# The first two blocks of rows handled in parts, and one transfer in place of two for the last weight rows

## The chip, the cores and the metric

The kernel runs on one NeuronCore of a Trainium2 chip. The metric is the device time of one execution in microseconds (us); lower is better. A NeuronCore has a matrix engine (PE, whose weight loads are shown apart as PEld), a vector engine (DVE), a scalar engine (ACT), GpSimd (POOL) and a sync engine (SP) that here only issues transfers. Each engine works through its own instruction list in order. DMA transfers are issued by SP, ACT and POOL, each on a queue of its own, and all queues are served by the same 16 DMA engines.

## The reference

```python
xn = layernorm(x)                                  # x = A_q, 2048 rows of 576
k_shift = sum_t k_pad[:, t:t+S] * shift_k[:, 3-t]  # causal convolution of 4 taps
kv = k_shift * v
y = irfft(rfft(kv, 2S) * rfft(ssm_k, 2S))[:S] + kv * ssm_D
out = x + xn * y + relu(xn @ w1) @ w2              # w1: 576 x 4608, w2: 4608 x 576
```

All data is float32. The feed-forward part (`relu(xn @ w1) @ w2`) is most of the work; the long convolution runs beside it.

## The kernel before, in words

The rows are taken in blocks of 512 (`BT` = 4 tiles of 128 rows). The first half of the rows is blocks 0 and 1, which are the tiles 0 to 3 and 4 to 7. The 4608 hidden columns are taken in 18 chunks of 256 (`FC`), each in two halves f = 0 and f = 1 of 128. Each chunk runs once for each half of the rows: 36 passes g.

To keep float32 precision every operand is split in a high part (cast to fp32r, named `hi`, `h` or index 0) and a low part (the difference, index 1). A product is then three matmuls: high by high, high by low, low by high. The 576 inputs are four pieces c = 0 to 3 of 128 and a rest of 64; for the rest the high and the low part of x lie one under the other in one operand of 128 partitions (`hl`), so the 64 rest rows of `w1` must stand twice over in `r1[:, 4, :]`.

The start (the first 33 us) is written out by hand:

- `load_acc` brings pairs of x tiles. The pair of tiles 0 and 1 and that of tiles 2 and 3 come first: each pair is two transfers of 64 partitions, one issued by SP and one by ACT. Then SP issues `load_w1(0)` (the weights of chunk 0, in four transfers), the pairs 4, 5 and 6, 7, and two `w2` tiles.
- `block_rows` centres the rows (`xn`), on DVE (statistics, then a subtraction: tiles 0, 2, and in block 1 tiles 4, 6, 7) or on ACT (tiles 1, 3 and 5).
- `block_xT` turns a block with PE transposes into PSUM tiles (`psx`: two tiles of two banks, and one `psf`), casts each piece on ACT to the high part (L304, rest L305) and subtracts it on DVE for the low part (L307, L308); then ACT copies the pieces out in float32 (`xf`) for later sums. `keep_warm` puts matmuls on nothing between the transposes.
- `split_w` casts weights to their high part on ACT (L529) and makes the low part on POOL (L530).
- `classical(g, b, f, ...)` writes the 14 matmuls of one half f of a chunk for block b: 12 on pieces, 2 on the rest. `hidden` makes the two parts of the relu on ACT (`hh`, L608) and DVE (`ll`, L613). For chunk 0, block 0 the order is `classical(0, 0, 0)`, then `classical(0, 0, 1)`, then the transposes of block 1 and the two halves of block 1; after them the first second-layer matmuls (`mm2`, tiles `pso`).

`tc.issue_after` fixes the order of two instructions on one engine without a wait. Passes 1 to 35 take their weights by `load_w1(g)` on POOL's queue, one pass ahead.

Of the kernel before, what the change touches and what calls it, by code (L numbers as in the profile page):

```python
# [12 lines left out]
AF = mybir.ActivationFunctionType  # L13
OP = mybir.AluOpType
# [3 lines left out]
P = 128  # L18
# [8 lines left out]
FT = 2  # L27
# [12 lines left out]
GR = P // (2 * A2)  # L40
NG = A1 // GR
N_WARM = 22
N_BETWEEN = 6
LATE = (0, 1, 5)


# [54 lines left out]
def h3_ffn_kernel(ctx: ExitStack, tc, x, k, v, shift_k, ssm_k, ssm_D, w1, w2, fwd, inv, mid, out):  # L101
# [41 lines left out]
    def fft_psum():  # L143
        return ps_f.tile([P, 512], F32, tag="f", name="psf")
# [17 lines left out]
    def halves(u):  # L162

        return slice(u * A1, (u + 1) * A1), slice((1 - u) * A1, (2 - u) * A1)
# [5 lines left out]
                with tc.issue_after(behind.ins):  # L170
                    behind = nc.sync.dma_start(kt_n[h, :, d:d + KD, :], src)

    def move(tile_, rows, t, store=False, queues=(nc.sync, nc.sync)):
        for u in range(U):
            a, b = tile_[halves(u)[0]], rows[u, :, t]
            last = queues[u].dma_start(*((b, a) if store else (a, b)))
        return last

# [95 lines left out]
    def block_rows(pool, b):  # L274

        xn = rows_tiles(pool, b)
        last = {t: done["low"] if b else None for t in (-2, -1)}
        for t in range(BT):
            last[t] = centre(xn[t], acc[b * BT + t], b * BT + t, CENTRED[b][t],
                             done["copied"] if b and t == 1 else last[t - 1 - (t < 3 or not b)])  # L280
        done["centred"] = last[BT - 1]
        return xn

    def block_xT(pool, b, names, tags, xn):

        wide = [ps_o.tile([P, 2, 512], F32, tag=f"o{k}", name=f"psx{b}{k}") for k in range(2)]
        ps = [wide[c // 2][:, c % 2, :] for c in range(4)] + [fft_psum()]
        if b == 0:
            transposed(ps, xn, [(c, t) for t in range(2) for c in range(5)])
            with tc.issue_after(done["pe"].ins):  # L290
                done["pe"] = keep_warm(N_BETWEEN)
            transposed(ps, xn, [(c, t) for c in range(5) for t in range(2, BT)])
        else:
            transposed(ps, xn, [(c, t) for c in range(5) for t in range(BT)])
        behind = done["centred"] if b == 0 else done["low"]
        for o, tag in zip(names, tags):
            operand(o, tag)
        rest_operand(b)
        with tc.issue_after(behind.ins):
            if b == 0:  # L300
                split_a(0)
            dst = [xo[names[c // 2]][:, :, c % 2, :] for c in range(4)]
            for c in range(4):
                nc.scalar.activation(dst[c][:, 0], ps[c], AF.Copy)  # L304
            high = nc.scalar.activation(hl[b][:64], ps[4][:64], AF.Copy)  # L305
            for c in range(4):
                nc.vector.tensor_tensor(dst[c][:, 1], ps[c], dst[c][:, 0], OP.subtract)  # L307
            done["low"] = nc.vector.tensor_tensor(hl[b][64:], ps[4][:64], hl[b][:64], OP.subtract)  # L308
        with tc.issue_after(high.ins):
            if b == 0:  # L310
                split_r(0)
                split_b(0)
                split_d(0)
            for o, src in zip(names, wide):
                xf[o] = pool.tile([P, 2, 512], F32, tag=f"xf{o}", name=f"xf{o}")
                nc.scalar.activation(xf[o], src, AF.Copy)  # L316
            xf[b] = pool.tile([64, 512], F32, tag=f"xfr{b}", name=f"xfr{b}")
            done["copied"] = nc.scalar.activation(xf[b], ps[4][:64], AF.Copy)
        if b:
            with tc.issue_after(done["low"].ins):  # L320
                for t in range(2 * BT):
                    if CENTRED[t // BT][t % BT] == "act":
                        stats(t, acc[t])
# [181 lines left out]
    def load_w1(g):  # L505
        queue = nc.gpsimd if g else nc.sync
        f = slice((g % NQ) * FC, (g % NQ + 1) * FC)
        r1 = wp.tile([P, 5, FC], F32, tag="r1", name=f"r1_{g}")
        for n in range(1 if g else 2):
            to = slice(0, FC) if g else slice(n * P, n * P + P)  # L510
            queue.dma_start(r1[:, :4, to], w1[:4 * P, f][:, to].rearrange("(c p) f -> p c f", p=P))
            if n == 0:
                for h in range(2):
                    queue.dma_start(r1[64 * h:64 * h + 64, 4, :], w1[4 * P:, f])
        raw1[g] = r1

    def load_w2(g, j):
# [7 lines left out]
    def split_w(g, kind, src, shape, bufs=1):  # L525
        w = wp.tile([P, 2, *shape], F32R, tag=kind, name=f"{kind}{g}", bufs=bufs)
        n = src.shape[1]
        with at_turn(g):
            nc.scalar.activation(w[:, 0, :n], src, AF.Copy)  # L529
        nc.gpsimd.tensor_tensor(w[:, 1, :n], src, w[:, 0, :n], OP.subtract)  # L530
        return w

# [86 lines left out]
    def classical(g, b, f, n_low, posted=0, upto=None):  # L619

        ps = bank(g, f, f"c{b}{f}")
        parts = ((wa[g], 0, wa[g], 2), (wb[g], 0, wd[g], 0))[f]
        names = (("00", "01"), ("10", "11"))[b]
        seq, late = [], []
        firsts, lasts = [], []
        for k in range(2):
            w, off = parts[2 * k:2 * k + 2]
            for c in range(2):
                h, l = w[:, 0, off + c, :], w[:, 1, off + c, :]
                hi, lo = xo[names[k]][:, 0, c, :], xo[names[k]][:, 1, c, :]  # L630
                seq += [(h, hi), (h, lo)]
                late.append((l, hi))
                if len(late) > LATE[n_low]:
                    seq.append(late.pop(0))
                if firsts:
                    firsts.insert(-1, (h, hi))
                    firsts.append((l, hi))
                else:
                    firsts = [(h, hi), (l, hi)]
                lasts.append((h, lo))  # L640
        if g == f == 0:
            seq, late = firsts + lasts, []
        seq.append((wr[g][:, 0, 0, f * P:(f + 1) * P], hl[b]))
        late.append((wr[g][:, 1, 0, f * P:(f + 1) * P], hl[b]))
        seq += late
        matmuls(ps, seq, True)
        tick(14 * W_MM)
        hidden(g, b, f, ps)
        post(posted, upto)

    def quad(g, units):

# [632 lines left out]

    warm = const.tile([P, 512], mybir.dt.bfloat16, name="warm")
    nc.vector.memset(warm, 0.0)
    for t in range(0, BT, 2):
        load_acc(t, queues=(nc.sync, nc.scalar))
    load_w1(0)  # L1290
    load_acc(BT)
    load_acc(BT + 2)
# [7 lines left out]
    def keep_warm(n):  # L1300
        for i in range(n):
            last = nc.tensor.matmul(idle[0], warm[:, :P], warm, start=True, stop=True)
        return last

    done["pe"] = keep_warm(N_WARM)
    with tc.tile_pool(name="fa", bufs=1) as fa:
        block_xT(fa, 0, ("00", "01"), (None, None), block_rows(fa, 0))
        xn = block_rows(fa, 1)
        classical(0, 0, 0, 1)
        classical(0, 0, 1, 2)  # L1310
        block_xT(fa, 1, ("10", "11"), ("s4", None), xn)
        load_w1(1)
        with tc.issue_after(done["low"].ins):
            inv_std(0, 2 * BT)
        with tc.issue_after(done["centred"].ins):
            for j in range(FT):
                split_w2(0, j)
                load_w2(1, j)
        classical(0, 1, 0, 0)
        split_a(1)  # L1320
        classical(0, 1, 1, 0)
        split_r(1)
        split_b(1)
        split_d(1)
        load_w1(2)
        spread_scales(fa)

        def unit(g, b, i, upto):
            mm2(g, b, i)
            post(1, upto)  # L1330

        for g in range(1, PLAIN):
            now = "00" if g < PLAIN - 1 else "10"
            for f in range(FT):
                for i in range(2):
                    unit(g - 1, 0, 2 * f + i, "00")
                if g == f == 1:
                    posts["at"] = second_half_of_start(fa)
                classical(g, 0, f, 0, 3, now if f else "00")
            for j in range(FT):  # L1340
                split_w2(g, j)
                load_w2(g + 1, j)
            for i in range(BT):
                unit(g - 1, 1, i, now)
            classical(g, 1, 0, 0, 3, now)
            split_a(g + 1)
            if g + 1 == PLAIN:
                sums(g + 1)
            split_r(g + 1)
            classical(g, 1, 1, 0, 3, None if g == PLAIN - 1 else now)  # L1350
            split_b(g + 1)
            split_d(g + 1)
            load_w1(g + 2)
        quad(PLAIN, [(PLAIN - 1, b, i) for b in range(2) for i in range(BT)])
        post(99)
# [38 lines left out]
```

## Time and profile before

| | |
|---|---|
| median of 3 runs | 1012.85 us (1012.47 to 1013.08) |
| the profiled execution, its own time | 1012.76 us |
| its span in the profile | 1011.0 us |
| PE busy | 1003.3 us (99%) |
| DVE, ACT, POOL busy | 685.9, 439.2, 442.5 us |
| POOL's rest-row transfers (L514) | 70, 36.7 us on POOL |

Between the span and the profiled execution's own time lie 1.8 us that the profile does not show. In the tables of stretches, each row gives for one stretch of the span the busy time and number of instructions of PE, PEld, DVE, ACT and POOL, the granted PE clock, the share of the 16 DMA engines, and GB/s. In timelines a row gives start, length, engine, line, operation, tiles, count, and in brackets the idle time before it with what ended it. In waits a row gives who waited for whom: total us, times, longest.

### The profile page before, as it was taken

Reading aid. Unit: us, or ns where it says so; the run is one execution under the profiler, and the core shown is the slowest. Engines: PE = TensorE matmul, PEld = TensorE weight load, DVE = VectorE, ACT = ScalarE, POOL = GpSimd, SP = SyncE. Lnnn points to the kernel's source line nnn. Section 1 sums busy time; section 2 is a strip of 40 time slices with the busy share of each in tenths; the row PEclk is TensorE's granted clock in tenths of the full one; section 3 lists DMA queues with packets and bytes.
Section 4 is the critical chain, followed back from the end, with each engine's and each line's share of the span. In section 5 each row is a group of like instructions: output and inputs, shape, how many; then the busy total and the mean of one; then the engine's idle time right before and its main releaser. Section 6 shows DMA issues by size and latency. Waiting matters only on the chain.

```text
span 1011.0 us, 17382 instructions
## 1 busy us (share of the span) xinstructions
PE 1003.3 (99%) x6502; PEld 844.4 (84%) x6502; DVE 685.9 (68%) x1057; ACT 439.2 (43%) x772; POOL 442.5 (44%) x500
## 2 busy tenths in 40 slices
PE   9999999999999999999999999999999999999998
PEld 5898999998878998898888888877777777787787
DVE  5787678875666676676767678556667666656774
ACT  7244444543554444444444444544454544432121
POOL 4335444554444744444444444334433244344450
PEclk9999999999999999999999999999999999999999
DMA  6654887771667534449863343478888987877954
GB/s 171 144 100 117 176 194 195 256 250 50 182 190 207 185 90 128 126 144 360 242 202 95 120 126 97 160 204 235 241 250 243 280 265 214 230 236 231 287 177 117
DMA packets 131032, 189.94 MB, mean 188 GB/s; under 512 B 69202, under 2 KB 83924, under 8 KB 130052
## 3 DMA queue, kind: packets, MB, share of 16 engines
q1 hardware_dynamic: 114564, 135.54, 47.0%
q0 software_dynamic: 15952, 52.40, 17.3%
q8 instruction: 51, 0.84, 0.3%
q10 hardware_dynamic: 432, 0.89, 0.3%
q14 instruction: 33, 0.27, 0.1%
HBM read 124.28 MB, written 50.34 MB: 173 GB/s over the span
## 4 chain that ended last, share of the span: by engine, by line
PE 97%; ACT 1%; DMA 1%; DVE 0%; issue 0%; ACTq 0%; DVEq 0%
PE pso L586 45%; PE psh L586 38%; PE psg L824 5%; PE psf L824 5%; PE psh_c L586 3%; DMA acc<-in_x 1%; ACT x L304 0%; DVE x L307 0%; PE psf L586 0%; ACT w L529 0%; ACT wb L529 0%; ACT xf L316 0%; ACT xs L224 0%; DVE bn L190 0%; ACT hh L608 0%
## 5 line engine op out<-in xcount | busy, mean ns | idle before, releaser
L586 PE MATMUL pso<-w,hh 128*128 128x288 f32 x2296 | 465.0, 296 | 0.0
L586 PEld LDWEIGHTS pso<-w,hh 128*128 128x128 f32 x2296 | 376.8, 188 | 30.8 <-ACT area L1134 6.5
L586 PE MATMUL pso<-w,ll 128*128 128x288 f32 x1148 | 338.4, 295 | 0.0
L811 DVE TENSOR_TENSOR acc<-pso,acc 128x576 f32<-128x576 f32 x237 | 178.7, 755 | 158.6 <-PE pso L586 158.2
L586 PEld LDWEIGHTS pso<-w,ll 128*128 128x128 f32 x1148 | 215.5, 188 | 0.0
L530 POOL TENSOR_TENSOR wb<-sums,wb 128x512 fp32r<-128x512 f32 x33 | 45.7, 1384 | 278.9 <-ACT wb L529 252.2
L530 POOL TENSOR_TENSOR w<-r,w 128x576 fp32r<-128x576 f32 x72 | 105.9, 1478 | 108.2 <-ACT w L529 107.9
L586 PE MATMUL psh<-xs,wb 128*128 128x512 f32 x396 | 102.4, 393 | 0.0
L586 PE MATMUL psh<-x,wa 128*128 128x512 f32 x396 | 102.2, 393 | 0.1
L613 DVE SCALAR_TENSOR_TENSOR ll<-psh,hh 128x512 fp32r<-128x512 f32 x66 | 45.5, 689 | 70.2 <-ACT hh L608 70.0
L586 PE MATMUL psh<-hl,wr 128*128 128x512 f32 x264 | 85.1, 403 | 0.0
L586 PEld LDWEIGHTS psh<-x,wa 128*128 128x128 f32 x396 | 72.4, 188 | 15.0 <-issue 0.4
L586 PEld LDWEIGHTS psh<-xs,wb 128*128 128x128 f32 x396 | 70.7, 188 | 12.1 <-issue 0.8
L711 ACT ACTIVATE psh<-psh 128x512 f32<-128x512 f32 x33 | 19.2, 582 | 137.7 <-DVE u L709 137.7
L530 POOL TENSOR_TENSOR wa<-r,wa 128x512 fp32r<-128x512 f32 x36 | 47.9, 1332 | 54.9 <-ACT wa L529 54.8
L824 PE MATMUL psg<-area 64*64 64x512 f32 (+10 forms) x632 | 64.1, 472 | 0.0
L586 PEld LDWEIGHTS psh<-hl,wr 128*128 128x128 f32 x264 | 46.0, 188 | 19.0 <-issue 10.4
L608 ACT ACTIVATE hh<-psh 128x512 fp32r<-128x512 f32 x66 | 39.2, 594 | 52.1 <-PE psh L586 51.8
L1114 DVE TENSOR_TENSOR area<-psf,area 128x512 f32<-128x512 f32 x72 | 44.7, 683 | 12.5 <-PE psf L824 8.1
L586 PE MATMUL psh<-x,wc 128*128 128x512 f32 x198 | 51.2, 394 | 0.0
L824 PE MATMUL psf<-area 64*64 64x512 f32 (+10 forms) x528 | 51.1, 451 | 0.0
L586 PE MATMUL psh<-xs,wc 128*128 128x512 f32 x198 | 51.0, 392 | 0.0
(144 smaller groups left out, 1436.2 us busy)
## 6 DMA issues: line engine op xcount, KB each, us to landing
r<-in_w POOLq DMA_DIRECT2D x70, 288.0 KB, 4.0
area<-area SPq DMA_DIRECT2D x144, 128.0 KB, 4.7
r<-in_w POOLq DMA_DIRECT2D x35, 512.0 KB, 4.9
zk<-area SPq DMA_DIRECT2D x64, 144.0 KB, 2.5
area<-zk SPq DMA_DIRECT2D x18, 512.0 KB, 4.6
area<-zx SPq DMA_DIRECT2D x18, 512.0 KB, 4.9
zy<-area SPq DMA_DIRECT2D x18, 512.0 KB, 2.9
area<-zy SPq DMA_DIRECT2D x32, 288.0 KB, 7.2
```

Source lines behind the costliest of these rows:

```text
L530: nc.gpsimd.tensor_tensor(w[:, 1, :n], src, w[:, 0, :n], OP.subtract)
L586: last = nc.tensor.matmul(ps, a, m, start=start and n == 0, stop=n == len(seq) - 1, skip_group_check=True)
L608: done["act"] = nc.scalar.activation(hh, ps, AF.Relu)
L613: done["ll"] = nc.vector.scalar_tensor_tensor(ll, ps, 0.0, hh, op0=OP.max, op1=OP.subtract)
L711: nc.scalar.activation(x, y, AF.Copy, scale=-1.0)
L811: done["acc"] = nc.vector.tensor_tensor(two(acc[t]), whole, two(acc[t]), OP.add)
L824: done["pe"] = nc.tensor.matmul(ps, a, m, start=start, stop=stop, skip_group_check=True)
L1114: nc.vector.tensor_tensor(filt[c][:, k, :], banks[k], filt[c][:, k, :], OP.mult)
```

## The change

What it does, part by part:

1. In `load_acc(2)` the second 64 partitions of the pair 2, 3 are loaded in two parts: 32 by ACT's queue, 32 by SP's.
2. `block_xT` gives each piece c = 0, 1, 2 a PSUM tile of its own (`psf`, half of a wide tile, `psf`); piece 3 and the rest share the second wide tile. The transposes of a block's first two tiles go first, for block 1 too; those of the last two go piece by piece, and the ACT cast and the DVE subtraction of a piece are written right behind its transposes. The `xf` copies are four of 512 columns, where there were two of 1024. `N_BETWEEN` goes from 6 to 3.
3. The high part of chunk 0's `wa` is made by DVE, where ACT made it.
4. The two halves of chunk 0 are written together (`first_chunk`), so that matmuls of the second half stand between those of the first. The casts of the first `w2` tiles on ACT move behind the casts of block 1.
5. In `load_w1` of every pass the 64 rest rows come by one transfer that reads them twice (its source has the dimensions 2, 64 and 256, the first with step 0), where two transfers of 64 rows came.

On PE, chunk 0 of block 0: `x_206` and `x_207` (after: `x_181`, `x_182`) are pieces 0, 1 and 2, 3 of block 0; `psh_c_260` is half f = 0, `psh_c_279` (after: `psh_c_261`) half f = 1; `hl` and `wr` are the rest. Before:

```order
L586 MATMUL psh_c_260<-x_206,wa_209 128x512 x2
L586 MATMUL psh_c_260<-x_207,wa_209 128x512 x2
L586 MATMUL psh_c_260<-hl_208,wr_222 128x512 x2
L586 MATMUL psh_c_279<-x_206,wb_225 128x512 x4
L586 MATMUL psh_c_279<-x_207,wd_228 128x512 x4
L586 MATMUL psh_c_279<-hl_208,wr_222 128x512
```

After:

```order
L599 MATMUL psh_c_260<-x_181,wa_197 128x512 x2
L599 MATMUL psh_c_260<-x_182,wa_197 128x512 x2
L599 MATMUL psh_c_261<-x_181,wb_223 128x512 x2
L599 MATMUL psh_c_261<-x_182,wd_226 128x512 x2
L599 MATMUL psh_c_260<-hl_183,wr_220 128x512 x2
L599 MATMUL psh_c_261<-x_181,wb_223 128x512 x2
```

Four matmuls of the second half now stand ahead of the two on the rest of the first half.

On ACT, between the relu parts of block 0 and the casts of block 1 (`w` is a `w2` tile, `x_321` or `x_302` is an operand of block 1). Before:

```order
L608 ACTIVATE hh_0_1_294<-psh_c_279 128x512
L529 ACTIVATE w_363<-r_0_0_123 128x576
L529 ACTIVATE w_368<-r_0_1_125 128x576
L304 ACTIVATE x_321<-psx_298 128x512 x2
L304 ACTIVATE x_322<-psx_299 128x512 x2
L305 ACTIVATE hl_323<-psf 64x512
```

After:

```order
L621 ACTIVATE hh_0_1_294<-psh_c_261 128x512
L307 ACTIVATE x_302<-psf 128x512
L307 ACTIVATE x_302<-psx_298 128x512
L307 ACTIVATE x_303<-psf 128x512
L307 ACTIVATE x_303<-psx_299 128x512
L307 ACTIVATE hl_304<-psx_299 64x512
L542 ACTIVATE w_335<-r_0_0_123 128x576
L542 ACTIVATE w_340<-r_0_1_125 128x576
```

The two `w2` casts moved behind the five casts of block 1.

On SP, the first transfers (`acc_109` is the pair 2, 3, `acc_117` the pair 4, 5, `r_0` chunk 0 of `w1`). Before:

```order
L176 DMA acc_109<-in_x 64x1152
L511 DMA r_0_112<-in_w 128x4x128
L514 DMA r_0_112<-in_w 64x256 x2
L511 DMA r_0_112<-in_w 128x4x128
L176 DMA acc_117<-in_x 64x1152 x2
```

After:

```order
L179 DMA acc_109<-in_x 64x1152
L177 DMA acc_109<-in_x 32x1152
L522 DMA r_0_113<-in_w 128x4x128
L524 DMA r_0_113<-in_w 128x1x256
L522 DMA r_0_113<-in_w 128x4x128
L179 DMA acc_117<-in_x 64x1152 x2
```

One x transfer is added ahead of the weights, and the rest rows are one row of the list.

```diff
-N_BETWEEN = 6
+N_BETWEEN = 3
...
-    def move(tile_, rows, t, store=False, queues=(nc.sync, nc.sync)):
+    def move(tile_, rows, t, store=False, queues=(nc.sync, nc.sync), part=A1):
         for u in range(U):
             a, b = tile_[halves(u)[0]], rows[u, :, t]
+            if u and part < A1:
+                queues[0].dma_start(a[part:], b[part:])
+                a, b = a[:part], b[:part]
             last = queues[u].dma_start(*((b, a) if store else (a, b)))
...
         wide = [ps_o.tile([P, 2, 512], F32, tag=f"o{k}", name=f"psx{b}{k}") for k in range(2)]
-        ps = [wide[c // 2][:, c % 2, :] for c in range(4)] + [fft_psum()]
-        if b == 0:
-            transposed(ps, xn, [(c, t) for t in range(2) for c in range(5)])
-            with tc.issue_after(done["pe"].ins):
-                done["pe"] = keep_warm(N_BETWEEN)
-            transposed(ps, xn, [(c, t) for c in range(5) for t in range(2, BT)])
-        else:
-            transposed(ps, xn, [(c, t) for c in range(5) for t in range(BT)])
+        ps = [fft_psum(), wide[0][:, 0, :], fft_psum(), wide[1][:, 0, :], wide[1][:, 1, :]]
...
+        transposed(ps, xn, [(c, t) for t in range(2) for c in range(5)])
+        if b == 0:
+            with tc.issue_after(done["pe"].ins):
+                done["pe"] = keep_warm(N_BETWEEN)
...
-            for c in range(4):
-                nc.scalar.activation(dst[c][:, 0], ps[c], AF.Copy)
-            high = nc.scalar.activation(hl[b][:64], ps[4][:64], AF.Copy)
-            for c in range(4):
-                nc.vector.tensor_tensor(dst[c][:, 1], ps[c], dst[c][:, 0], OP.subtract)
-            done["low"] = nc.vector.tensor_tensor(hl[b][64:], ps[4][:64], hl[b][:64], OP.subtract)
+        for cs in ((0,), (1,), (2,), (3, 4)):
+            transposed(ps, xn, [(c, t) for c in cs for t in range(2, BT)])
+            with tc.issue_after(behind.ins):
+                for c in cs:
+                    to = dst[c][:, 0] if c < 4 else hl[b][:64]
+                    high = nc.scalar.activation(to, ps[c][:to.shape[0]], AF.Copy)
+                for c in cs:
+                    if c < 4:
+                        nc.vector.tensor_tensor(dst[c][:, 1], ps[c], dst[c][:, 0], OP.subtract)
+                    else:
+                        done["low"] = nc.vector.tensor_tensor(hl[b][64:], ps[c][:64], hl[b][:64],
+                                                              OP.subtract)
...
             if n == 0:
-                for h in range(2):
-                    queue.dma_start(r1[64 * h:64 * h + 64, 4, :], w1[4 * P:, f])
+                queue.dma_start(r1[:, 4, :], w1[4 * P:, f].unsqueeze(0).to_broadcast([2, 64, FC]))
...
-        with at_turn(g):
-            nc.scalar.activation(w[:, 0, :n], src, AF.Copy)
+        if g == 0 and kind == "wa":
+            nc.vector.tensor_copy(w[:, 0, :n], src)
+        else:
+            with at_turn(g):
+                nc.scalar.activation(w[:, 0, :n], src, AF.Copy)
...
+    def first_chunk(b):
...
+        matmuls(ps[0], mixed(0), True)
+        if b == 0:
+            matmuls(ps[0], late[0], False)
+            matmuls(ps[1], high[1], True)
+            matmuls(ps[0], rests[0], False)
+            hidden(0, b, 0, ps[0])
+            matmuls(ps[1], late[1] + low[1] + rests[1], False)
+        else:
+            matmuls(ps[1], mixed(1), True)
+            matmuls(ps[0], late[0] + rests[0], False)
+            hidden(0, b, 0, ps[0])
+            split_a(1)
+            matmuls(ps[1], late[1] + rests[1], False)
+        tick(28 * W_MM)
+        hidden(0, b, 1, ps[1])
...
-    for t in range(0, BT, 2):
-        load_acc(t, queues=(nc.sync, nc.scalar))
+    load_acc(0, queues=(nc.sync, nc.scalar))
+    load_acc(2, queues=(nc.sync, nc.scalar), part=A1 // 2)
...
-        classical(0, 0, 0, 1)
-        classical(0, 0, 1, 2)
+        first_chunk(0)
         block_xT(fa, 1, ("10", "11"), ("s4", None), xn)
...
-        classical(0, 1, 0, 0)
-        split_a(1)
-        classical(0, 1, 1, 0)
+        first_chunk(1)
```

In `first_chunk`, for each half f: `mixed` is the eight matmuls on the high part of x (high weights, and low weights one step behind), `late` the four on its low part, `rests` the two on the rest; `high` and `low` are the two halves of `mixed`.

More of the change, by code (lines that the diff above doesn't have):

```diff
@@ L280, in block_rows @@
                              done["copied"] if b and t == 1 else last[t - 1 - (t < 3 or not b)])
-        done["centred"] = last[BT - 1]
+        done["centred"], done["moved"] = last[BT - 1], last[BT - 2]
         return xn
@@ L298, in block_xT @@
         rest_operand(b)
-        with tc.issue_after(behind.ins):
-            if b == 0:
-                split_a(0)
-            dst = [xo[names[c // 2]][:, :, c % 2, :] for c in range(4)]
-            for c in range(4):
-                nc.scalar.activation(dst[c][:, 0], ps[c], AF.Copy)
-            high = nc.scalar.activation(hl[b][:64], ps[4][:64], AF.Copy)
-            for c in range(4):
-                nc.vector.tensor_tensor(dst[c][:, 1], ps[c], dst[c][:, 0], OP.subtract)
-            done["low"] = nc.vector.tensor_tensor(hl[b][64:], ps[4][:64], hl[b][:64], OP.subtract)
+        transposed(ps, xn, [(c, t) for t in range(2) for c in range(5)])
+        if b == 0:
+            with tc.issue_after(done["pe"].ins):
+                done["pe"] = keep_warm(N_BETWEEN)
+            with tc.issue_after(done["moved"].ins):
+                split_a(0)
+        dst = [xo[names[c // 2]][:, :, c % 2, :] for c in range(4)]
+        for cs in ((0,), (1,), (2,), (3, 4)):
[10 more added lines that the diff above has]
+                                                              OP.subtract)
+        done["high"] = high
         with tc.issue_after(high.ins):
@@ L313, in block_xT @@
                 split_d(0)
-            for o, src in zip(names, wide):
+            if b:
+                for j in range(FT):
+                    split_w2(0, j)
+                    load_w2(1, j)
+            for o in names:
                 xf[o] = pool.tile([P, 2, 512], F32, tag=f"xf{o}", name=f"xf{o}")
-                nc.scalar.activation(xf[o], src, AF.Copy)
+            for c in range(4):
+                nc.scalar.activation(xf[names[c // 2]][:, c % 2, :], ps[c], AF.Copy)
             xf[b] = pool.tile([64, 512], F32, tag=f"xfr{b}", name=f"xfr{b}")
@@ L624, in classical @@
         seq, late = [], []
-        firsts, lasts = [], []
         for k in range(2):
@@ L634, in classical @@
                     seq.append(late.pop(0))
[L635 to L642, printed above, removed]
         seq.append((wr[g][:, 0, 0, f * P:(f + 1) * P], hl[b]))
@@ L649, in classical, with mixed @@
         post(posted, upto)
+    def first_chunk(b):
+        names = (("00", "01"), ("10", "11"))[b]
+        ps, high, low, late, rests = [], [], [], [], []
+        for f in range(FT):
+            ps.append(bank(0, f, f"c{b}{f}"))
+            w = [((wa[0], 0, wa[0], 2), (wb[0], 0, wd[0], 0))[f][2 * k:2 * k + 2] for k in range(2)]
+            at = [(w[c // 2][0], w[c // 2][1] + c % 2, xo[names[c // 2]][:, :, c % 2, :])
+                  for c in range(4)]
+            high.append([(v[:, 0, o, :], x[:, 0]) for v, o, x in at])
+            low.append([(v[:, 1, o, :], x[:, 0]) for v, o, x in at])
+            late.append([(v[:, 0, o, :], x[:, 1]) for v, o, x in at])
+            rests.append([(wr[0][:, n, 0, f * P:(f + 1) * P], hl[b]) for n in range(2)])
+        def mixed(f):
+            h, l = high[f], low[f]
+            return [h[0], h[1], l[0], h[2], l[1], h[3], l[2], l[3]]
+        matmuls(ps[0], mixed(0), True)
[13 more added lines that the diff above has]
+        hidden(0, b, 1, ps[1])
     def quad(g, units):
@@ L1314, in h3_ffn_kernel @@
             inv_std(0, 2 * BT)
[L1315 to L1318, printed above, removed]
-        classical(0, 1, 0, 0)
-        split_a(1)
-        classical(0, 1, 1, 0)
+        first_chunk(1)
         split_r(1)
```

## The prediction

> **What bounds the kernel now.** I read the page first (its busy shares and the chain that ended last), then a table of stretches, then the waits and timelines of the one stretch in which PE is not full.
>
> ```profile
> span 1011.0 us, 17382 instructions
> ...
> PE 97%; ACT 1%; DMA 1%; DVE 0%; issue 0%; ACTq 0%; DVEq 0%
> ```
>
> ```profile
> 0.00:33.00 33.00, 30.42 (x149) 20.87 (x150) 21.50 (x53) 22.09 (x42) 13.55 (x24) 1.00 0.59 148
> 33.00:200.00 167.00, 166.90 (x995) 151.24 (x994) 124.97 (x209) 68.53 (x128) 76.53 (x80) 1.00 0.69 172
> ...
> 400.00:600.00 200.00, 200.00 (x1306) 175.79 (x1305) 143.42 (x209) 90.74 (x163) 91.65 (x102) 1.00 0.57 177
> ```
>
> PE carries 97% of the chain and from 33 us on it has no gap. So a gain in the first 33 us reaches the end whole, and nothing that only relieves DVE, ACT or POOL later can show. The question is when the first second-layer weight load (`pso<-w,hh`) starts: 29.47 us now. The start by PE's weight loads, where waits show best (a busy PE hides short ones under modelled ends):
>
> ```profile
> 10.77 0.86 PEld L245 LDWEIGHTS psx<-ident,xn 128*128 128x128 f32 x8 [0.57 <-DVE xn L259]
> ...
> 12.12 0.19 PEld L586 LDWEIGHTS psh_c<-x,wa 128*128 128x128 f32 x1 [0.30 <-ACT x L304]
> ...
> 13.59 1.22 PEld L586 LDWEIGHTS psh_c<-x,wa 128*128 128x128 f32 x6 [0.19 <-ACT x L304]
> 15.13 0.19 PEld L586 LDWEIGHTS psh_c<-x,wa 128*128 128x128 f32 x1 [0.32 <-DVE x L307]
> 15.91 0.30 PEld L586 LDWEIGHTS psh_c<-hl,wr 128*128 128x128 f32 x2 [0.59 <-ACT xf L316]
> ...
> 19.47 0.49 PEld L245 LDWEIGHTS psx<-ident,xn 128*128 128x128 f32 x3
> 20.67 1.40 PEld L245 LDWEIGHTS psx<-ident,xn 128*128 128x128 f32 x13 [0.72 <-DVE xn L259]
> ...
> 22.48 1.00 PEld L586 LDWEIGHTS psh_c<-x,wa 128*128 128x128 f32 x5
> ...
> 25.90 0.30 PEld L586 LDWEIGHTS psh_c<-hl,wr 128*128 128x128 f32 x2 [0.53 <-DVE hl L308]
> ...
> 27.64 1.33 PEld L586 LDWEIGHTS psh_c<-x,wd 128*128 128x128 f32 x6
> 29.01 0.42 PEld L586 LDWEIGHTS psh_c<-hl,wr 128*128 128x128 f32 x2
> 29.47 0.42 PEld L586 LDWEIGHTS pso<-w,hh 128*128 128x128 f32 x2
> ```
>
> The waits are for casts, for low parts, and at 20.67 for the last centred tile of block 1. The engines behind them:
>
> ```profile
> 10.20 0.52 DVE L259 TENSOR_SCALAR xn<-acc,mv 128x576 f32<-128x576 f32 x1
> 12.59 2.49 DVE L307 TENSOR_TENSOR x<-psx,x 128x512 fp32r<-128x512 f32 x4 [1.87 <-ACT x L304]
> 15.11 0.69 DVE L308 TENSOR_TENSOR hl<-psf,hl 64x512 fp32r<-64x512 f32 x1
> ...
> 17.36 0.81 DVE L190 BATCH_NORM_STATS2 bn<-acc 128x6 f32<-128x288 f32 x2
> ...
> 20.10 0.52 DVE L259 TENSOR_SCALAR xn<-acc,mv 128x576 f32<-128x576 f32 x1
> ```
>
> ```profile
> 10.58 0.61 ACT L529 ACTIVATE wa<-r 128x512 fp32r<-128x512 f32 x1
> 11.47 2.07 ACT L304 ACTIVATE x<-psx 128x512 fp32r<-128x512 f32 x4 [0.28 <-PE psx L245]
> ...
> 14.48 0.42 ACT L529 ACTIVATE wd<-r 128x256 fp32r<-128x256 f32 x1
> ...
> 20.40 1.25 ACT L529 ACTIVATE w<-r 128x576 fp32r<-128x576 f32 x2
> 21.55 2.05 ACT L304 ACTIVATE x<-psx 128x512 fp32r<-128x512 f32 x4
> ```
>
> **The change part by part.** Times are us from the span's start.
>
> *x of tiles 2 and 3.* Its last part lands here (chain, in order of time):
>
> ```profile
> 1.37 7.63 DMA acc<-in_x
> ```
>
> That is 9.0. The same 1.18 MB of x stand ahead of the weights; only 147 KB change queues. At the 243 GB/s quoted below these are 0.6 us, the most it can gain; the most it can lose is one more issue on SP, 0.47 us (row below). Near rows favour neither end: I take 0.
>
> *`wa` by DVE.* DVE does it at 10.7, in the 1.87 us in which it waits for ACT. A 128x512 cast lies between the 0.52 of the one-source row and the 0.62 of a two-source one (2.49 for four): hidden, and ready by 11.4 for the first product at 11.9. POOL then starts its low part no later than before. Cost 0.
>
> *Piece by piece.* ACT began when four transposes were through; now two do, 0.11 each (0.86 for eight): 11.47 becomes 11.25. Casts follow each other by 0.49 ((2.07 - 0.6)/3), the first is done at 11.86. DVE began after the second cast (12.59) and now begins after the first, 11.87: 0.72 earlier. Its row of work up to block 1's last centred tile is unbroken (15.11 to 20.62), so that tile comes at 19.90 if its data is there.
>
> *Order of the matmuls, block 0.* The last cast that PE waits for (13.59) is done at 13.37; 23 matmuls are left, 0.23 each (six in 27.64 to 29.01). The low parts come in time (piece 3 by 14.4, needed 14.6), `wb` and `wd` by 14.7 (needed 14.9), the rest by 15.1 (needed 15.8). End: 13.37 + 22 x 0.23 + 0.1 = 18.5 instead of 19.47.
>
> *Block 1.* With the tile at 19.90, transposes from 19.95, the first cast at 20.43: the `w2` casts no longer stand ahead (21.55 before). Ten transposes end at 21.05, the last cast at 22.5, 23 matmuls left: 22.53 + 5.06 + 0.1 = 27.7. That is 1.77 before 29.47 and 7.8 after the tile. The moved `w2` casts end at 24.1 and POOL's low parts at some 26.4, ahead of 27.7; if block 1 comes later they come later with it. Four `xf` copies for two cost ACT about 0.1, behind the casts, hidden. Three warm matmuls fewer free PE while it waits for DVE anyway (0.57 idle at 10.77): 0.
>
> *The rest rows.* This decides. Rows on how a transfer is shared among the DMA engines, for two transfers on ACT's queue of 64 partitions, and for two of 8 (each: the queue's packets, MB, share):
>
> ```profile
> q10 hardware_dynamic: 160, 0.59, 17.1%
> ...
> acc<-in_x ACTq DMA_DIRECT2D x2, 288.0 KB, 7.6
> ```
>
> ```profile
> q10 hardware_dynamic: 32, 0.00, 0.5%
> ...
> scale_n<-sq ACTq DMA_DIRECT2D x2, 1.0 KB
> ```
>
> Eighty packets each are 64 rows and 16 completions; sixteen each are 8 rows and 8 completions. So the outermost dimension limits the shares: 16 engines for 64, 8 for 8. The new transfer reads from a source whose outermost dimension is 2, into 128 partitions. No row shows two sides that differ. If the smaller side counts, two engines move 64 KB each, where sixteen moved 8 KB each, and on SP's queue the second half of `w1` and tiles 4 to 7 stand behind them. Prices per engine, from 4 to 16 us and from 310 to 314 us (nearly all 1152-byte packets):
>
> ```profile
> DMA packets 1904, 2.92 MB, mean 243 GB/s; under 512 B 194, under 2 KB 1346, under 8 KB 1904
> ```
>
> ```profile
> q1 hardware_dynamic: 695, 0.71, 52.3%
> ```
>
> The first is 15.2 GB/s an engine, 64 KB in 4.3; the second 0.71 MB/(0.523 x 4 us x 16) = 21.2 GB/s, 3.1. The 1024-byte rows are nearest to the second. Less the 0.4 to 0.5 of the share they had, the two engines fall behind by 2.7 (up to 3.8). The last x transfer was issued at 9.0:
>
> ```profile
> L176 SPq DMA_DIRECT2D acc<-in_x x1: 465/465/465, 9.0 to 9.0; - x1
> ...
> DMA to landing us min/median/max: 7.5/7.5/7.5
> ```
>
> It landed at 16.5, the slowest engine's time. The average engine: 3.01 MB at 243 GB/s from 2.2 on is 14.6; with some 0.7 from last packet to landing, an estimate, 15.3. With the two engines as average ones the tiles 6 and 7 land at 18.0 (16.5 + 3.8 = 20.3 at worst), where DVE now could use them at 16.65 (17.36 less 0.72). So the wait moves from the casts to this transfer: statistics at 18.05, 3.26 to the last tile (17.36 to 20.62) gives 21.3, plus 7.8 is 29.1. `w1`'s second half comes at about 14, little later than ACT wants it.
>
> By the Trainium skill, "DMA: Bandwidth & Descriptors", section "Why a DMA increments its semaphore by 16 and not by 1", the number of engines is the largest up to 16 that divides the outermost dimension of both sides, and "Rules for kernel authors" warns of a leading zero-stride broadcast of c copies. By that rule the sum is 1012.5; with 16 engines it is 1011.1. The two rows agree with it for equal sides.
>
> *The 35 other passes.* POOL issues one transfer less in each:
>
> ```profile
> L514 POOL DMA_DIRECT2D r<-in_w x70 | 36.7, 530 | 1.7 <-DMA area<-in_shift_k 1.0 <-issue 0.7
> ```
>
> 35 x 0.53 = 18.5 us less on POOL, which PE never waits for: 0. Slower landings there are covered by loading a pass ahead; the exception is the third rival.
>
> **Sum.** 0 + 0 for the loads of x and for `wa`, -1.77 for the start as planned, +1.4 given back to the late tiles: 29.47 to 29.1, so 1012.76 - 0.37 = 1012.4 for the profiled execution. The median stands 0.09 above that execution: 1012.5.
>
> **The rivals.** A change of under 0.2% (2.0 us) cannot be told from none here.
>
> *First: sixteen engines serve the transfer after all.* For it: the destination has 128 partitions. Against it: the completions of the 8-row transfers. The start is then as planned, 1011.1, with 0.4 either way from the x of tiles 2 and 3 and from waits on each cast; more is stopped by tiles 6 and 7 landing at 16.5.
>
> *Second: the two engines are also the slowest, or the price is 4.3.* The tiles land at up to 20.3: 23.6 + 7.8 = 31.4, 1.9 later than now, 1014.8. It still counts as no change.
>
> *Third, slower: the rest rows on POOL's queue.* There too two engines at a time would move 64 KB each, 3.1 us, 35 times, and the convolution's exchanges on SP's queue must share these engines. They have no slack at places:
>
> ```profile
> PEld psf L824 <- DMA area<-area: 1.7, 6, 0.3
> ```
>
> Six times PE's weight load was released by such a transfer. One full collision costs PE up to 3.1, six of 0.4 cost 2.4; from 2.4 on, with the start's -0.4, the kernel is slower by 0.2%. Five collisions would end near 1016. Against it: transfers take turns on an engine, and POOL's may be shared out otherwise.
>
> **How the numbers follow.** The forecast with the second rival has 0.58 (1011.9 to 1014.8, all within 0.2%), the first rival 0.28, of which 0.12 lie under 1010.8, the third 0.14. So faster 0.12, same 0.58 + 0.16 = 0.74, slower 0.14. The range takes in nearly all of the first rival and of the forecast: 1010.7 to 1014.3.
>
> **What would show it.** First casts at 11.25 and DVE's low parts at 11.9 show the piecewise step; the rest products of block 0 behind four of the second half, without a wait, the order. A DVE or ACT wait for `acc` at 16 to 18 and the first `pso` weight load near 29 show the two engines; no such wait and 27.7 show the first rival; PE waits for DMA after 250 us the third. It would be wrong if the granted clock fell below 1.00 in PE's gap before 21.3, or if the low parts of `wa` or `wb` came late on POOL.

## The result, and the profile after

| | before | after |
|---|---|---|
| median | 1012.87 us (1012.04 to 1014.42) | 1021.51 us (1019.95 to 1028.26) |
| profiled execution, its span | 1012.76, 1011.0 us | 1019.98, 1018.2 us |
| first `pso` weight load | 29.47 us | 30.62 us |

The changed kernel is slower: ratio 1.0097, 95% interval 1.0072 to 1.0122. The forecast was no change. The page of the changed kernel (span; the chain that ended last, by engine):

```profile
span 1018.2 us, 17314 instructions
...
PE 87%; DMA 7%; DVE 2%; ACT 1%; POOL 1%; issue 1%; SPq 1%; DVEq 0%; POOLq 0%; ACTq 0%
```

PE carried 97% of that chain before; now transfers hold 7% of it. A table of stretches of the changed kernel, and the one row of before that differs most from it:

```profile
0.00:33.00 33.00, 29.25 (x138) 19.77 (x139) 21.10 (x50) 21.86 (x45) 12.13 (x22) 1.00 0.58 148
33.00:150.00 117.00, 116.91 (x695) 105.86 (x695) 84.56 (x151) 46.20 (x86) 52.67 (x52) 1.00 0.68 148
150.00:360.00 210.00, 207.88 (x1473) 180.23 (x1473) 143.14 (x218) 93.75 (x177) 101.02 (x107) 1.00 0.62 186
360.00:470.00 110.00, 110.00 (x712) 96.97 (x711) 76.04 (x115) 49.10 (x89) 50.54 (x52) 1.00 0.47 142
470.00:570.00 100.00, 98.72 (x640) 86.24 (x639) 70.19 (x98) 46.76 (x85) 45.22 (x47) 1.00 0.70 214
570.00:780.00 210.00, 210.00 (x1368) 170.88 (x1368) 141.30 (x207) 96.12 (x158) 82.45 (x83) 1.00 0.64 180
780.00:850.00 70.00, 68.73 (x441) 52.37 (x440) 43.46 (x66) 34.74 (x54) 24.87 (x25) 1.00 0.90 253
```

```profile
150.00:360.00 210.00, 210.00 (x1489) 183.08 (x1488) 145.07 (x220) 95.06 (x178) 105.12 (x118) 1.00 0.60 188
```

PE, full from 33 us on before, now loses 2.1, 1.3 and 1.3 us in three stretches, and nothing between them. With the 1.15 us of the start that is 5.8 of the 7.2 us of span; the other 1.4 is in PE's busy time (1004.6 against 1003.3 us), where short waits can lie under modelled ends.

The start of the changed kernel: PE's weight loads, then DVE.

```profile
15.52 0.30 PEld L599 LDWEIGHTS psh_c<-x,wb 128*128 128x128 f32 x2 [1.13 <-ACT wb L542]
...
22.97 0.14 PEld L248 LDWEIGHTS psf<-ident,xn 128*128 128x128 f32 x1 [1.39 <-DVE xn L262]
...
30.62 0.41 PEld L599 LDWEIGHTS pso<-w,hh 128*128 128x128 f32 x2
```

```profile
11.45 0.69 DVE L310 TENSOR_TENSOR x<-psf,x 128x512 fp32r<-128x512 f32 x1 [1.04 <-ACT x L307]
...
18.25 0.82 DVE L193 BATCH_NORM_STATS2 bn<-acc 128x6 f32<-128x288 f32 x2 [3.47 <-DMA acc<-in_x]
...
22.40 0.52 DVE L262 TENSOR_SCALAR xn<-acc,mv 128x576 f32<-128x576 f32 x1
```

DVE starts its low parts earlier than before (11.45 against 12.59), then stands 3.47 us before tile 4's statistics, since that tile has not landed. Two rows of stretches show what the DMA engines do then and a little later:

```profile
17.00:18.00 1.00, 1.00 (x6) 0.81 (x5) 0.00 (x0) 1.00 (x3) 0.71 (x1) 1.00 0.11 32
...
22.00:25.00 3.00, 2.02 (x12) 1.45 (x13) 2.93 (x7) 1.66 (x4) 0.00 (x0) 1.00 0.13 42
```

A DMA share of 0.11 to 0.13 is what two engines of sixteen make (0.125): from 17 to 18 us on the x tiles queued behind chunk 0's rest rows, from 22 to 25 us mostly on the rest rows of the next pass, of whose 0.13 MB some 0.11 move in this stretch. The share alone does not tell two busy engines from sixteen that are mostly idle; the runs with more copies, below, do. The chain that ended last has the x transfer of tiles 4 and 5 in it (first row), and then transfers of the convolution and, in the last row, of the weights, of which the chain of before has none (start, duration):

```profile
7.42 10.74 DMA acc<-in_x
...
161.51 8.33 DMA area<-rows_n
...
292.43 6.67 DMA zk<-area
...
333.60 10.00 DMA area<-in_k
...
480.28 10.31 DMA r<-in_w
```

And PE's own waits (total us, times, longest) are those for engines that work on the convolution and on the passes in turn:

```profile
PE psh L599 <- ACT psh L749: 1.3, 2, 0.8
PE psh L599 <- ACT p L732: 1.3, 1, 1.3
...
PE pso L599 <- DVE area L946: 1.1, 1, 1.1
```

None of these waits is for a transfer. A late transfer holds up DVE or ACT, which work in order, and behind the held instruction stands the relu or the copy that PE needs.

### The profile page after: what moved, and what is told of

Read it like the earlier page. It is cut to its first block, busy times and chain, and to the rows that moved or that the text cites. A ratio compares the mean times of both kernels' runs of the same rounds, so it can differ in the third digit from the quotient of the medians.

```text
span 1018.2 us, 17314 instructions
## 1 busy us (share of the span) xinstructions
PE 1004.6 (99%) x6499; PEld 844.3 (83%) x6499; DVE 683.7 (67%) x1058; ACT 439.0 (43%) x775; POOL 434.6 (43%) x465
## 4 chain that ended last, share of the span: by engine, by line
PE 87%; DMA 7%; DVE 2%; ACT 1%; POOL 1%; issue 1%; SPq 1%; DVEq 0%; POOLq 0%; ACTq 0%
PE pso L599 41%; PE psh L599 34%; PE psg L862 5%; PE psf L862 4%; PE psh_c L599 3%; DMA acc<-in_x 1%; DMA area<-rows_n 1%; DMA r<-in_w 1%; DMA area<-in_k 1%; DMA area<-zx 1%; DMA zk<-area 1%; DMA area<-area 0%; DMA area<-in_shift_k 0%; SPq L467 0%; SPq L179 0%
```

## The experiments

"The two transfers" are the loop of before over 64 rows; all kernels but one start from the changed one. A time is a median; the kernel before ran beside each and had 1012.9 to 1013.4.

### Undoing the one transfer: everywhere, in chunk 0, in the passes; and doing it alone

`two_back` has this edit; `two_first` makes it for g = 0 only, `two_later` for g > 0 only, and `one_alone` is the kernel before with the reverse edit.

```diff
-                queue.dma_start(r1[:, 4, :], w1[4 * P:, f].unsqueeze(0).to_broadcast([2, 64, FC]))
+                for h in range(2):
+                    queue.dma_start(r1[64 * h:64 * h + 64, 4, :], w1[4 * P:, f])
```

> All parts of the change but the one transfer of the rest rows; each pass loads them by two transfers of 64 rows again. Theory A (the one transfer is carried by two DMA engines only; it makes tiles 4 to 7 late and delays the convolution's exchanges): start as planned, first second-layer weight load at about 27.7 us, no PE wait after 100 us, 1011.1 us. Rival B (the new order of the start costs by itself what is lost there): first second-layer weight load at 30 us or later, 1013.5 or more. Rival C (the runs scatter for another reason, such as where the loads fall in POOL's list): PE still waits after 100 us, 1015 or more.

> Two transfers again for chunk 0 alone (SP's queue); the 35 later passes keep the one transfer. Theory A: the start as planned (27.7 us to the first second-layer weight load), but the PE waits after 100 us stay, some 6 us of them: about 1017 us. Rival B: 30 us or later at the start, about 1020 us.

> Two transfers again for the 35 later passes (POOL's queue); chunk 0 keeps the one transfer. Theory A: tiles 4 to 7 stay late and the first second-layer weight load stays near 30.6 us, no PE wait after 100 us: about 1014.0 us. Rival C (POOL's list, not the engines that carry the transfer): PE waits after 100 us in this kernel too, 1018 or more.

> The kernel before with the one transfer of the rest rows in every pass as its only edit. Theory A: tile 4 is centred no earlier than 18.2 us as in the changed kernel, so the last centred tile comes at about 22.9 instead of 20.6 and the first second-layer weight load at about 31.7; with some 6 us of PE waits after 100 us that is about 1021 us. Rival B (the loss at the start belongs to the new order): the start stays at 29.5, about 1019 us.

| | one transfer in | us | ratio to before (95%) |
|---|---|---|---|
| `two_back` | nothing | 1011.25 | 0.998 (0.9971 to 0.9989) |
| `two_later` | chunk 0 | 1015.58 | 1.0027 (1.0017 to 1.0036) |
| `two_first` | 35 passes | 1022.68 | 1.009 (1.0069 to 1.0111) |
| `one_alone` | all, old start | 1023.28 | 1.0108 (1.0091 to 1.0124) |

Without the one transfer the rest of the change is a gain of 0.2%, and this version is faster than both kernels. Its DVE, PE and stretch rows:

```profile
14.85 0.82 DVE L193 BATCH_NORM_STATS2 bn<-acc 128x6 f32<-128x288 f32 x2
...
19.00 0.52 DVE L262 TENSOR_SCALAR xn<-acc,mv 128x576 f32<-128x576 f32 x1
```

```profile
27.21 0.41 PEld L600 LDWEIGHTS pso<-w,hh 128*128 128x128 f32 x2
```

```profile
150.00:360.00 210.00, 209.54 (x1476) 181.47 (x1475) 142.86 (x219) 95.00 (x178) 105.41 (x118) 1.00 0.59 186
```

Tile 4 is there when DVE comes to it. The first `pso` load is 2.26 us earlier than before, but the span (1009.8) only 1.2: of this difference 0.46 is a PE gap at 150 to 360 us that the kernel before has not. That PE, so much earlier, meets the convolution there would explain the gap; this was not tried, and the other 0.6 us stay open.

`two_first` keeps the good start (27.22) and loses in the three stretches of the changed kernel:

```profile
150.00:360.00 210.00, 206.68 (x1463) 179.03 (x1462) 139.93 (x213) 94.99 (x178) 102.47 (x109) 1.00 0.62 188
...
470.00:570.00 100.00, 98.81 (x632) 85.46 (x632) 69.97 (x98) 45.62 (x82) 47.12 (x49) 1.00 0.68 207
...
780.00:850.00 70.00, 67.38 (x434) 51.21 (x434) 42.51 (x63) 33.08 (x51) 25.63 (x26) 1.00 0.88 250
```

So rival B falls: the start costs nothing without the slow transfer, and the passes lose with it alone. Rival C's other cause, POOL's list, is not settled by these four, since the list is shorter in just the kernels that lose in the passes; `pairs2` and `wide128`, below, part the two. The size was missed: 11.4 us above `two_back`, where 6 were expected, and 7.9 of span even between the profiled runs. The three longest of the six runs of `two_first` have a mean granted clock of 0.996 or 0.997, the others 0.999. `two_later` has no PE wait in the passes, but its start was later than the changed kernel's: 32.21. While PE stood waiting for the late tiles its granted clock fell:

```profile
23.00:25.00 2.00, 1.61 (x8) 1.57 (x9) 2.00 (x4) 1.09 (x3) 0.00 (x0) 0.58 0.04 8
25.00:28.00 3.00, 3.00 (x12) 2.45 (x11) 2.67 (x5) 2.87 (x6) 0.66 (x1) 0.71 0.00 0
```

In the changed kernel's profile it stayed at 1.00 there. From the last centred tile to `pso` `two_later` needs 8.87 us, the changed kernel 7.70. `one_alone`: DVE gets tile 4 at 18.18, `pso` loads at 31.85 (31.7 expected). The old start ends later, but it loses less by the one transfer: 2.4 us against the kernel before, where the new start loses 3.4 against `two_back`. The parts do not add: 4.3 and 11.4 apart, 10.3 together. The fallen clock of `two_later` is 1.2 us of this, and the runs of `two_first` and of the changed kernel overlap. A later start also leaves the convolution more time, which would explain the rest; that was not tried by itself.

### Is it the number of engines? Copies and transfers

The transfer reads 128/c rows c times, c = 4, 8, 16: same bytes, rows and instructions (below for c = 4). The products on the rest rows are then other ones, so these kernels are for their times alone.

```diff
-    w1[4 * P:, f].unsqueeze(0).to_broadcast([2, 64, FC])
+    w1[4 * P:4 * P + 32, f].unsqueeze(0).to_broadcast([4, 32, FC])
```

> The changed kernel, but the one transfer reads 32 rest rows four times over, not 64 twice: the same bytes, rows and number of transfers (the products on the rest rows are other ones). Theory A (as many engines as copies): each of four engines moves 32 KB, so they fall behind by 4.6 x (32 - 8)/(64 - 8) = 2.0 us instead of 4.6; the first second-layer weight load at about 28.6 us, half or less of the PE waits after 100 us, 1013 to 1017 us. Rival C (the form of one transfer for two, its place in POOL's list or the repeated reading costs, not the engines): as the changed kernel, 1019 or more.

> As copies4, with 16 rows read eight times. Theory A: eight engines move 16 KB each and fall behind by 0.7 us; first second-layer weight load at 27.2 to 27.6, hardly a PE wait after 100 us, 1011.3 to 1012.5 us. Rival C: 1019 or more.

> As copies4, with 8 rows read sixteen times: still one transfer in each pass and a source of repeated reads. Theory A: sixteen engines, nobody falls behind, as with two transfers: first second-layer weight load at 27.2 us, 1011.3 us. Rival C: 1019 or more.

Measured 1018.19, 1014.14 and 1012.76 us, after 1021.51 with two copies; all three are 1 to 2 us above what theory A expected. The first `pso` load of the three, in this order:

```profile
29.81 0.41 PEld L599 LDWEIGHTS pso<-w,hh 128*128 128x128 f32 x2
```

```profile
28.55 0.41 PEld L599 LDWEIGHTS pso<-w,hh 128*128 128x128 f32 x2
```

```profile
27.09 0.42 PEld L599 LDWEIGHTS pso<-w,hh 128*128 128x128 f32 x2
```

The time falls with each doubling of the copies, at the start down to `two_back`'s 27.2, so the number of engines is the cause there and repeated reads are not. With four and eight copies it was about 1.2 us later than expected: the price per KB taken from two copies does not hold for smaller shares. The last x transfer landed at 19.6, 18.8, 17.7 and 15.8 us with 2, 4, 8 and 16 copies, and at 16.0 in `two_back`; so with two copies it was 3.6 us late, not the 4.6 that the expectations start from. POOL's queue shows the steps too (packets, for 2, 4, 8 and 16 copies):

```profile
q0 software_dynamic: 23232, 52.53, 18.1%
```

```profile
q0 software_dynamic: 18752, 52.46, 17.8%
```

```profile
q0 software_dynamic: 16512, 52.42, 17.2%
```

```profile
q0 software_dynamic: 15392, 52.40, 17.1%
```

Per pass these are 224, 96, 32 and 0 packets more than with sixteen copies.

Sixteen copies still scatter, from 1010.55 to 1016.27 us. The profiled one (1014.83) lost some 2.3 us of PE before 340 us, with all sixteen engines in use for the rest rows. PE's wait, then DVE, then POOL:

```profile
PE psh L599 <- ACT psh L749: 2.3, 1, 2.3
```

```profile
335.12 3.83 DVE L555 TENSOR_TENSOR sums<-sums,r 128x256 f32<-128x256 f32 x2
```

```profile
336.00 1.43 POOL L543 TENSOR_TENSOR w<-r,w 128x576 fp32r<-128x576 f32 x1
337.38 1.27 POOL L543 TENSOR_TENSOR wa<-r,wa 128x512 fp32r<-128x512 f32 x1
```

The two sums take 0.88 us in `two_back`; here the second ends only behind POOL's two subtractions, and the DVE step behind it is what ACT's copy for PE waits for. By the Trainium skill, "SBUF — State Buffer", section "SBUF: two separate sides", DVE with two SBUF inputs and GpSimd hold a shared pair of ports one at a time, each for a whole instruction. The rows fit that, with 3.38 us in place of 0.42 for the second sum.

I took POOL's shorter list for what moves the two together (theory D), and tried it with two transfers (`pairs2`, `pairs16`) and with one of 128 different rows (`wide128`):

```diff
-                queue.dma_start(r1[:, 4, :], w1[4 * P:, f].unsqueeze(0).to_broadcast([2, 64, FC]))
+                for h in range(2):
+                    queue.dma_start(r1[64 * h:64 * h + 64, 4, :],
+                                    w1[4 * P:4 * P + 32, f].unsqueeze(0).to_broadcast([2, 32, FC]))
```

```diff
-    w1[4 * P:, f].unsqueeze(0).to_broadcast([2, 64, FC])
+    w1[3 * P + 64:, f]
```

> The changed kernel with two transfers of 64 partitions in each pass again, so that POOL's list is as long as before, but each reads 32 rest rows twice over, so its source has the outermost dimension 2 (other products on the rest rows). Theory A1 (in the later passes too, the two engines alone cost): two engines per transfer, 32 KB each; if both transfers go to the same two engines, all as in the changed kernel, 1019 or more, with the first second-layer weight load near 30.6 us. If they go to different ones, as with four copies, 1015 to 1018. Theory D (part of the loss of the passes comes from POOL's shorter list, which puts POOL's weight splits on top of DVE's sums, a DVE operation of 0.42 us that takes 3 us near 335 to 346 us): no stretched DVE operation of over 2.3 us there, and 2 to 4 us less than the changed kernel, 1017 to 1019.

> As pairs2, but each of the two transfers reads 4 rest rows sixteen times. Sixteen engines and POOL's list as before: theories A and D both say 1011.3 us, first second-layer weight load at 27.1, and no run over 1013. If reading the same rows many times costs by itself, 1012.8 and scatter up to 1016 as with one transfer of sixteen copies.

> The changed kernel, but the one transfer reads 128 different rows of w1 (448 to 575) once each: one transfer, sixteen engines, no repeated reads (other products on the rest rows). Theory D: as one transfer of sixteen copies, about 1012.8 us, some runs at 1014 to 1016 with a DVE sum stretched to 3 us near 335 us, some at 1011. Repeated reads as the cause of that scatter: 1011.3 and no run over 1013.

`pairs2` gave 1018.43, `pairs16` (4 rows, sixteen times) 1010.85, `wide128` 1011.42 us. So two transfers are no cure if each is carried by two engines, and one is harmless if sixteen carry it: a shorter list on POOL is neither needed for the loss nor enough for it. But `pairs2` is 3.1 us below the changed kernel, as theory D said and theory A1 (1019 or more) did not. POOL's list was not as before in it: POOL spent 48.7 us on issuing the 70 transfers, 36.7 in the kernel before. What the 3.1 us come from stays open. `pairs2` starts as late as the changed kernel:

```profile
30.95 0.42 PEld L601 LDWEIGHTS pso<-w,hh 128*128 128x128 f32 x2
```

On SP's queue, then, the two transfers delayed the rest as one of twice the size does, as if both fell on the same two engines. A DVE addition, 0.75 us elsewhere, was still stretched, which theory D excluded:

```profile
343.51 2.44 DVE L1041 TENSOR_TENSOR area<-area 128x576 f32<-128x576 f32 x1
```

The changed kernel has one of 2.48 us at 344.13 us. Theory D stays open at best: over 1014 us came 2 of 12 runs of `wide128` and 4 of 10 of `copies16`, against 0 of 18 of `two_back` and `pairs16`, but also 1 of 10 of `two_nosplit` and 1 of 11 of `two_oldorder` (below), which have two transfers.

A gap of PE in these runs cost more than its length. In the profile of `copies16` the granted clock was 0.66 from 340 to 345 us, behind the gap. The four runs of `copies16` over 1014 us have a mean clock of 0.998, the six others 0.999 or more; of `copies4` four of five have 0.997 or 0.998. The profiled run of `copies8` is the longest of its ten (1019.03 us), with sums of 3.80 us and a clock of 0.55 from 345 to 350 us; only its start is used here.

### Parts of the start

From `two_back`: the pair of tiles 2, 3 loaded as before (`two_nosplit`), and chunk 0's matmuls in the old order with the new casts (`two_oldorder`; the lines of `classical` that make the old order within a half come back too and are left out below).

```diff
-    load_acc(2, queues=(nc.sync, nc.scalar), part=A1 // 2)
+    load_acc(2, queues=(nc.sync, nc.scalar))
```

```diff
...
-        first_chunk(0)
+        classical(0, 0, 0, 1)
+        classical(0, 0, 1, 2)
...
-        first_chunk(1)
+        classical(0, 1, 0, 0)
+        split_a(1)
+        classical(0, 1, 1, 0)
```

> Two transfers of the rest rows in every pass, and the pair of tiles 2 and 3 loaded as before, by two transfers of 64 partitions. If loading its second half in two parts brought these tiles 0.5 us earlier, the first casts and the first second-layer weight load come 0.5 us later than in the kernel with two transfers and the split (27.7 instead of 27.2; 1011.7 us). If that was only the scatter between runs, 27.2 and 1011.3 us.

> Two transfers of the rest rows in every pass, the new casts and PSUM tiles, but the matmuls of chunk 0 in the order of before, half by half. Theory A: from the last centred tile to the first second-layer weight load there are 8.5 to 8.9 us again instead of 7.7, so the weight load comes at 28.0 to 28.4 and the time is 1012.0 to 1012.4. If the new casts alone bring the operands in time, 27.2 and 1011.3.

`two_nosplit`: 1011.16 us, first `pso` load at 26.99. The split load is worth nothing: DVE gets tile 2 at 8.46 here and at 8.55 in `two_back`, both earlier than in the kernel before (9.10), so that difference is not the split's. `one_early`, which has the split, gets the tile at 9.05. `two_oldorder`: 1012.25 us (ratio 0.999, 0.9981 to 0.9999), DVE and PE:

```profile
18.74 0.52 DVE L262 TENSOR_SCALAR xn<-acc,mv 128x576 f32<-128x576 f32 x1
```

```profile
27.59 0.42 PEld L600 LDWEIGHTS pso<-w,hh 128*128 128x128 f32 x2
```

From the last centred tile (19.26) to `pso` 8.33 us: 7.69 with the new order (19.52 to 27.21), 8.85 before (20.62 to 29.47). With the new order it is 7.69 to 7.71 in every trace but that of `two_later`. So the order is worth 0.64; the other 0.5 belongs to what else differs, the casts by piece and the moved `w2` casts above all, which no run parts. With 8.5 to 8.9 expected, the order is worth a little less than thought. In the medians the order's share, 1.0 us, is no more than their intervals.

### Where in the passes

```diff
-                queue.dma_start(r1[:, 4, :], w1[4 * P:, f].unsqueeze(0).to_broadcast([2, 64, FC]))
+                if 0 < g < 14:
+                    queue.dma_start(r1[:, 4, :], w1[4 * P:, f].unsqueeze(0).to_broadcast([2, 64, FC]))
+                else:
+                    for h in range(2):
+                        queue.dma_start(r1[64 * h:64 * h + 64, 4, :], w1[4 * P:, f])
```

This is `one_early`; `one_late` has `g >= 14`.

> Two transfers for chunk 0; one transfer of two copies (two engines) in the passes 1 to 13, whose weights are loaded up to 340 us, and two transfers after that. Theory A (the two engines delay the convolution's exchanges at the few places where PE ends up waiting for them): PE waits only between 150 and 360 us, some 3 to 5 us of them in all, 1014 to 1016 us. If the loss of the passes is instead spread evenly over them (a cost of each pass), 13 of 35 passes: 1011.3 + 13/35 x 11.4 = 1015.5 with waits all along up to 340.

> The other way about: one transfer of two copies only in the passes 14 to 35, loaded after 340 us. Theory A: no PE wait before 360 us, PE waits at 480 to 560 and 800 to 840 us alone, 3 to 6 us, 1014 to 1017 us, and together with the early passes about the 11.4 us of all of them. Spread evenly: 1011.3 + 22/35 x 11.4 = 1018.5 with PE waits in most passes.

`one_early` 1017.21 us (1015.57 to 1022.16), `one_late` 1014.10 (1012.31 to 1018.46). Two stretches of the early one, and the same two of the late one:

```profile
150.00:360.00 210.00, 204.30 (x1446) 176.22 (x1445) 139.77 (x213) 92.42 (x174) 101.52 (x108) 1.00 0.61 184
...
470.00:570.00 100.00, 100.00 (x650) 87.64 (x649) 70.70 (x101) 47.15 (x85) 46.40 (x51) 1.00 0.67 214
```

```profile
150.00:360.00 210.00, 209.44 (x1476) 181.24 (x1475) 142.34 (x219) 94.79 (x178) 105.86 (x117) 1.00 0.59 187
...
470.00:570.00 100.00, 98.65 (x630) 85.23 (x629) 69.61 (x100) 44.60 (x82) 47.55 (x49) 1.00 0.66 195
```

The early passes cost 5.7 us of PE between 150 and 360 us (3 to 5 expected) and nothing elsewhere in the passes; the late ones leave that stretch as in `two_back` and cost 1.35 at 470 to 570 and 0.5 behind it. Both theories had put the time of `one_early` lower, at 1016 at most; what parts them is the place. The 11.4 us are not a price of each pass: PE loses them in the same few stretches, where its next work hangs on an exchange. Both halves together (6.0 and 2.9 above `two_back`) make 8.8 of the 11.4; the rest is within the scatter of `two_first` (1018.74 to 1026.23).

## Why the prediction was wrong

The step that failed is **the 35 other passes**, priced at 0 because weights are loaded a pass ahead. PE itself waited for weights no longer than 0.7 us in all (0.4 before), but the exchanges on the same engines were late, and so, once, were weights for ACT. Before it cast `wa` at 490.68 us ACT stood 3.14 us for the transfer issued at 480.28, and the copy that PE waited for next (L732, 1.3 us) stood behind the cast. In `two_back` ACT stood 0.87 us there. The third rival had this mechanism, place and sign, but a chance of 0.14 and a size of some 3 us. Its row counted exchanges that PE's weight loads waited for, 0.3 us at most. That row is unchanged in the changed kernel (1.7 us, 6 times, 0.3): the waits that grew are those of ACT and DVE, which hold PE's operands up second-hand. The largest, changed kernel and then before (`two_back` has 4.9, 2, 3.4):

```profile
ACT area L944 <- DMA zk<-area: 14.5, 4, 7.4
```

```profile
ACT area L906 <- DMA zk<-area: 3.8, 2, 3.4
```

Those were to be asked for slack. The convolution's reads of `rows_n` (L467) show the size (min/median/max us to landing, changed kernel, then `two_back`):

```profile
DMA to landing us min/median/max: 2.1/2.9/8.5
```

```profile
DMA to landing us min/median/max: 2.0/3.1/4.8
```

The median is as good as in `two_back`. The worst one is 3.7 us later, and it is the one that the chain waits for. That is about the two engines' time for 64 KB: 32 GB/s at a share of 0.11 (17 to 18 us) is 18 GB/s an engine, which makes 3.6 us, an estimate. The worst landing goes with the number of engines: 8.0, 7.9, 8.4 and 7.3 us in the other traces with two engines there (`one_alone`, `two_first`, `one_early`, `pairs2`), 6.5 with four (`copies4`), 5.6 with eight (`copies8`), and 4.8 to 5.6 with sixteen, in nine traces.

The saving on POOL was mis-sized too, at no cost: one transfer with two copies takes POOL 0.85 us to issue, each of the two took 0.53, so 7.1 us were saved and not 18.5.

**The rest rows in chunk 0**: two engines, as forecast. Mis-sized was whom they delay. The sum moved tiles 6 and 7 by 1.5 us; but everything behind the transfer passes those two engines: `w1`'s second half (a PE wait of 1.13 us, which the later wait for the tile covers) and tile 4, used at 18.25 in place of 14.85. The last centred tile came at 22.92 (21.3 forecast) and `pso` 7.70 later (7.8). The delay was nearer the upper bound: the last x transfer landed 3.6 us later than in `two_back` (19.6 against 16.0), where 2.7 was taken and 3.8 was the most.

**The start without it** held. First cast 10.85 (11.25 forecast), first low part 11.48 (11.87), last tile 19.52 (19.90), `pso` 27.21 (27.7): every one 0.4 to 0.5 early, as the tiles 2 and 3 were. The end was 1011.25 against the first rival's 1011.1, which is in part luck: the start won more than planned, and of its 2.26 us only 1.2 reached the end of the profiled run, where the prediction let a gain of the first 33 us reach the end whole. `wa` by DVE (10.08, 0.42 us) and the split load cost nothing, as said; so did three warm matmuls fewer, as far as one can tell beside the rest.

The rule of the Trainium skill that the prediction weighed ("DMA: Bandwidth & Descriptors", section "Why a DMA increments its semaphore by 16 and not by 1") agrees with the runs: the last x transfer landed 3.8, 3.0 and 1.9 us later with 2, 4 and 8 copies than with sixteen. The sum by it, 1012.5, was the forecast itself and had the same faults.

## What to carry to other kernels

Before two transfers are merged into one, look at the outermost dimension of both sides: here a leading repeat of two left fourteen of sixteen DMA engines out, and what was queued behind waited for the other two. A transfer that nobody waits for still has a price if its engines also carry one that somebody does; ask of every engine that waits for transfers, not only of the bounding one, how much slack it has and what stands behind it. The transfer saved was worth nothing here, even with sixteen engines for the one that was left: 1011.42 us (`wide128`) against 1011.25 (`two_back`).

## What the hardware showed that was not expected

- Two transfers in a row from SP, each for two engines, delayed the start as one of twice the size does (`pairs2`, 30.95 us to `pso`, one transfer 30.62), as if through the same two.
- On POOL's queue a transfer for fewer engines has more packets: 224 more a pass with two engines than with sixteen, 96 with four, 32 with eight. POOL also needs longer to issue one: 0.85 us with two copies, 0.57 with sixteen.
- After the waits for tiles 4 to 7 the granted clock of PE fell to 0.58 in `two_later` (1.7 us of PE idle between 20 and 25 us) and stayed at 1.00 in the changed kernel (1.3) and in `one_alone` (2.2).
- After gaps near 340 us it fell to 0.66 (`copies4`, `copies16`) and 0.55 (`copies8`) for some 5 us.
- A DVE addition of 0.42 us took 3.38 beside two POOL subtractions of the weights.
